# Weight conversion in pairs of slices, with the low parts formed by TensorE

## The chip, the cores and the metric

The kernel runs on one core of one Trainium2 chip. The metric is the device time of one execution in microseconds. The kernel before was timed in three runs: 685.75, 686.35 and 686.82 us, median 686.35. One execution was taken by the hardware profiler. Engines are named as in the profile: PE is TensorE's matmul (PEld its weight load), DVE is VectorE, ACT is ScalarE, POOL is GpSimd, SP is SyncE, which here issues nearly all transfers.

## The reference

The first stage is a linear attention with a complex decay, step by step over the sequence; the second is a feed-forward layer over its output.

```python
batch, n_heads, seq, head_dim = (4, 8, 768, 48)
n_tokens, d_model, d_ff = (3072, 384, 2048)

mag = np.sqrt(a_re * a_re + a_im * a_im)
scale = np.minimum(mag, 0.999) / (mag + 1e-06)
a_re_n, a_im_n = (a_re * scale, a_im * scale)
for t in range(S):
    ar, ai = (a_re_n[:, :, t, :, None], a_im_n[:, :, t, :, None])
    new_re = ar * S_re - ai * S_im
    new_im = ar * S_im + ai * S_re
    kv = np.einsum('bhd,bhe->bhde', k[:, :, t], v[:, :, t])
    S_re, S_im = (new_re + kv, new_im)
    y[:, :, t] = np.einsum('bhd,bhde->bhe', q[:, :, t], S_re)

h = x @ w_in          # x: y as (3072, 384)
g = np.maximum(0.01 * h, h)
out = g @ w_out
```

The two weight matrices come in as float64, 384 x 2048 and 2048 x 384.

## The kernel before

**Attention.** The sequence is cut into 6 chunks of 128 steps. A sub-step is one chunk of two of the four batches; there are 12, numbered n. For each, `prep(n)` normalises the decays and forms their running products, mostly on DVE with some steps on ACT (lines L422 to L540). It multiplies q and k by them into a tile `qkt` (L521, L533), which five transfers per real or imaginary part (L549, L553, L557) bring into the layout `t96` that PE needs. Then `attend(n, bi)` handles the two batches one by one: transposes (L588), scores (L601), the mask on DVE (L605), outputs and old state (L626), the new state (L639). The output is split into a high part `xh` (fp32r, ACT, L628) and a low part `xl` (DVE, L631).

**Feed-forward.** Two attended units, 256 tokens, make a group; there are 12 groups. `moe(g)` goes through the 2048 hidden columns two blocks of 128 at a time. `mm1` forms 18 matmuls into one of two PSUM buffers `ph` (L679 to L681: high by high, low by high, high by low part). ACT and DVE turn it into `gh` and `gl` (L685 to L688), and `mm2`, one step behind, adds 18 matmuls into three output buffers `po` (L696, L697, L702). At the end ACT copies them out (L715) and SP sends them (L716).

**Weights.** They arrive as 64-bit words, 32 slices of 128 x 384: 16 of `w_in`, 16 of `w_out`, in turn. `load_weights` makes an fp32 value of each slice: two bit operations on DVE (L378, L382), a conversion of the lower word on ACT (L385), an add on POOL (L386) into `wcv`. ACT rounds it to the high part (L387), and POOL subtracts that to get the low part (L388). Two `cvt` buffers hold slices under way. The raw words lie in buffers borrowed from other tiles (`a`, `kn`, `xh`, `xl`, and `stg`, which is also the output tile); from the tenth slice on, three of them rotate. Each slice is one transfer on SP (L323).

**What sets the order.** No order is written by hand. A scheduler gives each engine's instructions a fixed order by simulating the program: an instruction is placed when its inputs and buffers are ready there, and the ready one with the lowest number of priority comes first. The first loads have 0, attention 1,000,000, feed-forward 2,000,000, preparation n 3,000,000 + 10,000 n, weights 3,005,000, so all weights rank between the first and second preparation. Tiles of one tag share the tag's buffers; a new tile waits until the old one has been read for the last time. On the chip each engine and each queue then works through its list in order.

After the last attention `check_weights` and `flag` test the input ranges; a general version of the program stands behind a branch and does not run here.

## Time and profile before

| | |
|---|---|
| median of three runs | 686.35 us |
| profiled execution | 686.39 us |
| its span, first to last instruction | 684.3 us |
| granted TensorE clock, mean | 0.990 |
| busy: PE, DVE, ACT, POOL | 577.0, 550.2, 364.8, 78.0 us |
| POOL, subtracts L388 | 16 x 1.375 us and 16 x 1.223 us |
| second attention's preparation ends on DVE (L533) | 125.5 us |
| last high part of the weights (L387) ends | 150.8 us |
| first output copy of the first group (L715) | 170.6 us |

Rows of the profile name the line, the engine, the operation, the tile written and the tiles read, the shape, and the count. A row of the timeline starts with its start and its duration in us, and ends, in brackets, with the idle time of the engine before it and what ended that. A row of the groups gives busy time in all, the mean of one in ns, and the idle time before them.

### The profile page before, as it was taken

To read this page: it belongs to the slowest core of one execution; us is meant where nothing else is said; L and a number is where in the kernel's file an instruction comes from. 1 tells how busy PE (TensorE), PEld (TensorE's weight loads), DVE (VectorE), ACT (ScalarE), POOL (GpSimd) and SP (SyncE) were. 2 spreads that over 40 slices of the span, in tenths; PEclk is the share of its full clock that TensorE was granted. 3 is DMA by queue.
4 is the path that set the end of the run, shared out by engine and by line. 5 is a ranking of instruction groups with operands and counts; after the bars stand their busy time and mean duration, and the time that the engine had idled before them with its cause. 6 is when DMAs were issued, how large, how long until landed. Compare 5 with 4: busy or idle time off the path is not lost.

```text
span 684.3 us, 14080 instructions
## 1 busy us (share of the span) xinstructions
PE 577.0 (84%) x5732; PEld 555.4 (81%) x5732; DVE 550.2 (80%) x915; ACT 364.8 (53%) x815; POOL 78.0 (11%) x75
## 2 busy tenths in 40 slices
PE   0000475899999999999999999999999998999996
PEld 0000365798999899899999999989999997999996
DVE  5999899999989799898989989989889885233331
ACT  6245256457457275473755727538366277583321
POOL 5645255450000000000000000000000000000000
PEclk9999999999999999999999999999999999899998
DMA  8231733630421703408034070251701748750000
GB/s 329 78 103 69 217 107 119 151 129 29 110 100 52 186 15 88 136 29 209 8 86 145 28 187 25 69 146 51 184 4 51 210 166 194 269 196 13 24 1 29
DMA packets 26232, 74.27 MB, mean 109 GB/s; under 512 B 3376, under 2 KB 9520, under 8 KB 26160
## 3 DMA queue, kind: packets, MB, share of 16 engines
q1 hardware_dynamic: 25552, 71.71, 35.1%
q10 hardware_dynamic: 608, 1.59, 1.0%
q8 instruction: 47, 0.77, 0.5%
q14 instruction: 25, 0.20, 0.1%
HBM read 49.55 MB, written 4.72 MB: 79 GB/s over the span
## 4 chain that ended last, share of the span: by engine, by line
PE 45%; DVE 29%; DMA 12%; ACT 5%; issue 4%; SPq 2%; POOL 1%; ACTq 0%; DVEq 0%; POOLq 0%
DMA t<-qkt 6%; PE po L696 6%; PE po L697 6%; PE po L702 5%; DMA wck<-in_w_dram 5%; PE ph L679 5%; PE ph L680 5%; PE ph L681 5%; PE px L626 4%; PE ps L601 4%; PE pu L639 3%; DVE tg L686 2%; DVE tmp L443 2%; DVE wcv L378 2%; DVE gl L688 2%
## 5 line engine op out<-in xcount | busy, mean ns | idle before, releaser
L679 PE MATMUL ph<-xh,win_hi 128*128 128x256 f32 x576 | 165.2, 287 | 6.7 <-DVE tg L686 5.2
L680 PE MATMUL ph<-xl,win_hi 128*128 128x256 f32 x576 | 164.6, 286 | 2.7 <-DVE xl L631 2.7
L681 PE MATMUL ph<-xh,win_lo 128*128 128x256 f32 x576 | 164.0, 285 | 0.0
L696 PE MATMUL po<-gh,wout_hi 128*128 128x256 f32 x576 | 145.6, 287 | 0.5 <-ACT gh L687 0.5
L697 PE MATMUL po<-gh,wout_lo 128*128 128x256 f32 x576 | 144.8, 286 | 0.0
L679 PEld LDWEIGHTS ph<-xh,win_hi 128*128 128x128 f32 x576 | 110.0, 191 | 8.5 <-DVE tg L686 6.5
L680 PEld LDWEIGHTS ph<-xl,win_hi 128*128 128x128 f32 x576 | 110.1, 191 | 3.5 <-DVE xl L631 2.9
L696 PEld LDWEIGHTS po<-gh,wout_hi 128*128 128x128 f32 x576 | 110.3, 192 | 1.8 <-ACT gh L687 1.0
L697 PEld LDWEIGHTS po<-gh,wout_lo 128*128 128x128 f32 x576 | 110.5, 192 | 0.2 <-issue 0.2
L681 PEld LDWEIGHTS ph<-xh,win_lo 128*128 128x128 f32 x576 | 110.0, 191 | 0.0
L686 DVE TENSOR_TENSOR tg<-ph,tg 128x512 f32<-128x512 f32 x96 | 65.8, 688 | 53.4 <-ACT tg L685 51.0
L685 ACT ACTIVATE tg<-ph 128x512 f32<-128x512 f32 x96 | 57.2, 595 | 92.0 <-PE ph L681 80.0
L588 PE MATMUL ptk<-ident,t 96*128 96x96 f32 x160 | 24.9, 265 | 79.4 <-DMA t<-qkt 79.1
L702 PE MATMUL po<-gl,wout_hi 128*128 128x256 f32 x576 | 89.8, 287 | 0.1
L688 DVE TENSOR_TENSOR gl<-tg,gh 128x512 fp32r<-128x512 f32 x96 | 66.5, 697 | 28.7 <-ACT gh L687 20.2
L588 PEld LDWEIGHTS ptk<-ident,t 96*128 96x128 f32 x160 | 17.9, 150 | 83.6 <-DMA t<-qkt 78.4
L687 ACT CAST gh<-tg 128x512 fp32r<-128x512 f32 x96 | 59.2, 619 | 48.6 <-DVE tg L686 41.6
L702 PEld LDWEIGHTS po<-gl,wout_hi 128*128 128x128 f32 x576 | 77.5, 192 | 0.5 <-DVE gl L688 0.3
L601 PE MATMUL ps<-t 96*128 96x128 f32 x384 | 59.1, 298 | 6.9 <-DVE xl L631 4.2
L601 PEld LDWEIGHTS ps<-t 96*128 96x128 f32 x384 | 53.1, 210 | 8.1 <-DVE xl L631 4.4
L443 DVE TENSOR_TENSOR tmp<-a 128x384 f32<-128x384 f32 x84 | 51.5, 613 | 1.4
L626 PE MATMUL px<-asb,v 128*32 128x128 f32 x768 | 48.4, 288 | 0.8 <-DVE asb L605 0.8
(118 smaller groups left out, 953.1 us busy)
## 6 DMA issues: line engine op xcount, KB each, us to landing
t<-qkt SPq DMA_DIRECT2D x44, 290.2 KB, 5.4
wck<-in_w_dram SPq DMA_DIRECT2D x10, 1152.0 KB, 5.7
a<-in_a_dram SPq DMA_DIRECT2D x12, 768.0 KB, 6.1
qk<-in_qk_dram SPq DMA_DIRECT2D x12, 768.0 KB, 4.8
v<-in_v_dram SPq DMA_DIRECT2D x12, 448.0 KB, 3.3
out_dram<-ot SPq DMA_DIRECT2D x12, 384.0 KB, 2.6
stage_xh<-in_w_dram SPq DMA_DIRECT2D x10, 384.0 KB, 3.0
stage_xl<-in_w_dram SPq DMA_DIRECT2D x10, 384.0 KB, 3.2
```

The costliest lines, as they stand in the source:

```text
L443: nc.vector.tensor_tensor(out=pr, in0=src.unsqueeze(2).to_broadcast([P, 2, 2, M]), in1=swap(ar, r), op=ALU.mult)
L601: nc.tensor.matmul(ps[:, h4], lhsT=t96[:, slot_of(1, h), bi, 0:C], rhs=t96[:, slot_of(0, h), bi, 0:C], start=True, stop=True)
L626: nc.tensor.matmul(px[32 * q : 32 * q + 32, i], lhsT=lhsT, rhs=rhs, start=first, stop=last)
L679: nc.tensor.matmul(o, lhsT=win_hi[:, k, fs], rhs=xh[:, k, :nt], start=(k == 0), stop=False)
L680: nc.tensor.matmul(o, lhsT=win_hi[:, k, fs], rhs=xl[:, k, :nt], start=False, stop=False)
L681: nc.tensor.matmul(o, lhsT=win_lo[:, k, fs], rhs=xh[:, k, :nt], start=False, stop=(k == TI - 1))
L686: nc.vector.tensor_tensor(out=tg[:, :w], in0=ph[:, :w], in1=tg[:, :w], op=ALU.max)
L687: nc.scalar.copy(gh[:, :w], tg[:, :w])
L688: nc.vector.tensor_tensor(out=gl[:, :w], in0=tg[:, :w], in1=gh[:, :w].bitcast(F32), op=ALU.subtract)
L696: nc.tensor.matmul(po[o][:, :nt], lhsT=wout_hi[:, f, os], rhs=gh[:, ts], start=(f == 0), stop=False)
L697: nc.tensor.matmul(po[o][:, :nt], lhsT=wout_lo[:, f, os], rhs=gh[:, ts], start=False, stop=False)
L702: nc.tensor.matmul(po[o][:, :nt], lhsT=wout_hi[:, f, os], rhs=gl[:, ts], start=False, stop=(f == NFC - 1))
```

## The change

Two neighbouring slices of one matrix are converted together, so 16 transfers, 16 conversions of twice the width, and 16 high parts take the place of 32. POOL keeps the add. Its subtract goes. In its place PE forms, for each slice, identity times the fp32 value plus negated identity times the high part in a PSUM buffer of the tag `h`, the one that `ph` uses (two buffers), and ACT copies the result out as the low part. The negated identity `nid` is a new tile, made once by ACT.

The raw words now lie in one `a` buffer, the `qkt` buffer (two pairs) and two buffers `ws` of their own, which rotate from the sixth pair on. `xh`, `xl`, `kn` and `stg` no longer hold raw words. Space for this comes from a smaller scratch area of the program (`dynamic_dma_scratch_size`) and from merging two small tiles.

The first 8 pairs keep their priority behind the first preparation. The other 8 are called from `moe(0)`, two for each of its first four steps, and get 3,015,000: behind the second preparation.

```diff
-STAGES = [
-    ("a", 3 * TI * 2 * C, 2), ("kn", H * 2 * D, 1), ("xh", TI * GT, 2), ("xl", TI * GT, 2), ("xh", TI * GT, 2),
-    ("xl", TI * GT, 2), ("stg", 2 * DM, 1),
-]
-AHEAD = 4
-EARLY = 8
-def STAGE_OF(i):
-    return i if i < 9 else 6 + i % 3
+NWS = 2
+STAGES = [("a", 3 * TI * 2 * C, 2), ("qkt", 4 * TI * 2 * (C + 1), 1)] + [("ws", 4 * DM, NWS)] * NWS
+AHEAD = 2
+EARLY = 4
+FIRST = 8
+NROT = NWS
+def STAGE_OF(i, n):
+    return i if i < n else n - NROT + (i - n) % NROT
...
+    nid = cp.tile([P, P], F32R, tag="nid", name="nid")
...
+    nc.scalar.activation(nid, ident, AF.Copy, scale=-1.0)
...
-            loaded[i] = stage[STAGE_OF(i)]
-            nc.sync.dma_start(out=loaded[i].bitcast(I64), in_=w_in[i // 2 + NFC * (i % 2)])
+            loaded[i] = stage[STAGE_OF(i, len(stage))]
+            s0 = i // 2 * 2 + NFC * (i % 2)
+            nc.sync.dma_start(
+                out=loaded[i].rearrange("p (s x) -> p s x", s=2).bitcast(I64),
+                in_=w_in[s0 : s0 + 2].rearrange("s p x -> p s x"),
+            )
...
+        for i in range(lo, hi):
+            f = i // 2 * 2
+            st = weight_dma(i)
+            cv = pp.tile([P, 2 * DM], I32, tag="cvt", name=f"wcv_{i}", bufs=2)
...
             nc.scalar.activation(lo_w, uwords[:, :, 0], AF.Copy, scale=2.0**-29)
             nc.gpsimd.tensor_tensor(out=cv, in0=hi_w, in1=lo_w, op=ALU.add)
             nc.scalar.activation(dh, wf, AF.Copy)
-            nc.gpsimd.tensor_tensor(out=dl, in0=wf, in1=dh.bitcast(F32), op=ALU.subtract)
+            for x in range(2):
+                pd = psh.tile([P, 512], F32, tag="h", name=f"pd_{i}_{x}")[:, 0:DM].rearrange("p (k x) -> p k x", k=TI)
+                nc.tensor.matmul(pd, lhsT=ident, rhs=wf[:, x], start=True, stop=False)
+                nc.tensor.matmul(pd, lhsT=nid, rhs=dh[:, x], start=False, stop=True)
+                nc.scalar.copy(dl[:, x], pd)
...
         for f in range(0, NFC, nf):
+            if g == 0:
+                load_weights(min(FIRST + f, NFC), min(FIRST + f + 2, NFC), PRIO_PREP + 15_000)
+                prio(PRIO_MOE)
             cur = mm1(f)
...
     load(0)
-    load_weights(0, EARLY // 2, PRIO_PREP + 5_000)
+    load_weights(0, EARLY, PRIO_PREP + 5_000)
...
         if n == 0:
-            load_weights(EARLY // 2, NFC, PRIO_PREP + 5_000)
+            load_weights(EARLY, FIRST, PRIO_PREP + 5_000)
...
-    nc = bacc.Bacc("TRN2", target_bir_lowering=False, num_devices=1)
+    nc = bacc.Bacc("TRN2", target_bir_lowering=False, num_devices=1, dynamic_dma_scratch_size=1024)
```

More of the change, by code (lines that the diff above doesn't have):

```diff
@@ L275, in body @@
     xacc = keep.tile([P, NT // C], F32, tag="xacc", name="xacc")
-    low = keep.tile([P, 4], F32, tag="low", name="low")
+    low = keep.tile([P, 5], F32, tag="low", name="low")
+    low, lnc = low[:, 0:4], low[:, 4:5]
     zfl = keep.tile([P, nsub, 2 * TI], F32, tag="zfl", name="zfl")
-    lnc = cp.tile([P, 1], F32, tag="lnc", name="lnc")
     wacc = keep.tile([P, 2, WCP * -(-NWC // WCK)], F32, tag="wacc", name="wacc")
@@ L313, in body @@
         st = pp.tile([P, size], I32, tag=t, name=f"stage_{t}_{len(stage)}", bufs=nb)
-        stage += [st[:, i * 2 * DM : (i + 1) * 2 * DM] for i in range(size // (2 * DM))]
-    s_next = [0]
+        stage += [st[:, i * 4 * DM : (i + 1) * 4 * DM] for i in range(size // (4 * DM))]
     raw = {}
@@ new lines, in load_weights @@
+        for i in range(lo, hi):
+            f = i // 2 * 2
+            st = weight_dma(i)
+            cv = pp.tile([P, 2 * DM], I32, tag="cvt", name=f"wcv_{i}", bufs=2)
+            if i % 2 == 0:
+                dh, dl = (
+                    x[:, :, f * P : (f + 2) * P].rearrange("p k (s x) -> p s k x", s=2) for x in (win_hi, win_lo)
+                )
+            else:
+                dh, dl = (x[:, f : f + 2].rearrange("p s (k x) -> p s k x", k=TI) for x in (wout_hi, wout_lo))
+            words = st.rearrange("p (x two) -> p x two", two=2)
+            uwords = st.bitcast(U32).rearrange("p (x two) -> p x two", two=2)
+            hi_w, lo_w = words[:, :, 1], words[:, :, 0]
+            wf = cv.bitcast(F32).rearrange("p (s k x) -> p s k x", s=2, k=TI)
+            nc.vector.tensor_scalar(
+                out=cv.bitcast(U32), in0=uwords[:, :, 1], scalar1=5, scalar2=2,
+                op0=ALU.logical_shift_left, op1=ALU.logical_shift_right,
+            )
+            nc.vector.scalar_tensor_tensor(
+                out=hi_w, in0=hi_w, scalar=-(1 << 30), in1=cv, op0=ALU.bitwise_and, op1=ALU.bitwise_or
+            )
+            nc.scalar.activation(lo_w, uwords[:, :, 0], AF.Copy, scale=2.0**-29)
+            nc.gpsimd.tensor_tensor(out=cv, in0=hi_w, in1=lo_w, op=ALU.add)
+            nc.scalar.activation(dh, wf, AF.Copy)
+            for x in range(2):
[3 more added lines that the diff above has]
+                nc.scalar.copy(dl[:, x], pd)
```

25 lines of the change are left out of this document (removed).

## The prediction

> **What bounds the kernel now.** I read the busy shares over the span first, then the busy time by stages. The first view has one digit per 17.1 us, the share of the slice in tenths; the second gives start and end, length, and the busy time (and instruction count) of each engine.
>
> ```profile
> PE   0000475899999999999999999999999998999996
> DVE  5999899999989799898989989989889885233331
> POOL 5645255450000000000000000000000000000000
> ```
>
> ```profile
> core 0: us, PE busy (x) PEld busy (x) DVE busy (x) ACT busy (x) POOL busy (x), PEclk, DMA share, GB/s
> 0.00:77.70 77.70, 0.80 (x2) 0.50 (x2) 67.67 (x97) 33.15 (x63) 41.16 (x43) 1.00 0.42 145
> 77.70:109.50 31.80, 21.92 (x146) 18.48 (x146) 28.46 (x45) 18.91 (x49) 15.02 (x14) 1.00 0.48 162
> 109.50:171.00 61.50, 54.46 (x467) 52.11 (x468) 57.82 (x91) 35.41 (x83) 21.79 (x19) 0.97 0.35 103
> 171.00:684.30 513.30, 499.77 (x5118) 484.32 (x5117) 396.30 (x685) 277.30 (x621) 0.00 (x0) 0.99 0.35 100
> ```
>
> From 171 us to the end PE is busy 499.8 of 513.3 us, so the end stands about 513 us behind the end of the first feed-forward group. What the change can move lies before 171: there PE does almost nothing for 77.7 us, idles 9.9 us of the next 31.8 and 7.0 us of the 61.5 after that. Over the same 77.7 us DVE is busy 67.7, and GpSimd (POOL) works only in those early stages. The timeline shows who releases PE (in brackets the idle time before it and its releaser).
>
> ```profile
> 69.81 1.82 DVE L533 TENSOR_TENSOR qkt<-qk,a 128x768 f32<-128x768 f32 x2
> 77.71 0.58 PE L588 MATMUL ptk<-ident,t 96*128 96x96 f32 x2 [73.12 <-DMA t<-qkt]
> 94.75 3.78 PE L601 MATMUL ps<-t 96*128 96x128 f32 x16 [4.15 <-DVE xl L631]
> 109.52 0.58 PE L680 MATMUL ph<-xl,win_hi 128*128 128x256 f32 x1 [2.65 <-DVE xl L631]
> 170.62 0.63 ACT L715 COPY ot<-po 128x256 f32<-128x256 f32 x2
> ```
>
> The first preparation ends on DVE at 71.6, its relay through DMA releases PE at 77.7, and two later idle stretches (4.15 and 2.65 us) wait for DVE again. The ramp is bound by DVE; L715 at 170.6 is the end of group 0. DVE is not only full, it is stretched while POOL works. The groups of 0 to 72 us come first (busy, mean ns), then the same forms from 180 to 540 us, where POOL is silent.
>
> ```profile
> L443 DVE TENSOR_TENSOR tmp<-a 128x384 f32<-128x384 f32 x8 | 7.4, 930 | 0.1
> L437 DVE TENSOR_TENSOR a<-a,tmp 128x1536 f32<-128x1536 f32 x2 | 4.8, 2405 | 0.0
> L446 DVE TENSOR_TENSOR a<-tmp 128x192 f32<-128x192 f32 x7 | 3.8, 548 | 0.1
> L378 DVE TENSOR_SCALAR wcv<-stage_xl 128x384 uint32<-128x384 uint32 x5 | 3.2, 638 | 0.0
> L378 DVE TENSOR_SCALAR wcv<-stage_xh 128x384 uint32<-128x384 uint32 x5 | 3.2, 634 | 0.9 <-POOL win_lo L388 0.9
> L528 DVE TENSOR_TENSOR qk<-qk,a 128x768 f32<-128x768 f32 x1 | 1.8, 1750 | 0.0
> L378 DVE TENSOR_SCALAR wcv<-stage_stg 128x384 uint32<-128x384 uint32 x3 | 1.1, 353 | 0.0
> ```
>
> ```profile
> L443 DVE TENSOR_TENSOR tmp<-a 128x384 f32<-128x384 f32 x61 | 33.9, 556 | 1.0
> L446 DVE TENSOR_TENSOR a<-tmp 128x192 f32<-128x192 f32 x61 | 21.6, 354 | 0.9
> L437 DVE TENSOR_TENSOR a<-a,tmp 128x1536 f32<-128x1536 f32 x8 | 14.0, 1755 | 0.0
> L528 DVE TENSOR_TENSOR qk<-qk,a 128x768 f32<-128x768 f32 x8 | 7.6, 955 | 0.0
> L423 DVE SCALAR_TENSOR_TENSOR tmp<-tmp 128x768 f32<-128x768 f32 x8 | 7.6, 948 | 0.0
> ```
>
> Excess, count by difference of means: L443 8 x 0.37 = 3.0; L437 2 x 0.65 = 1.3; L446 7 x 0.19 = 1.4; L378 10 x 0.28 = 2.8 against its unstretched 0.353; L528 0.8. That is 9.3 us in 28 of the window's 87 DVE instructions. The rest hold single stretched ones like L528, so I take 16 us as an estimate for the whole stage: above 9.3, and well below the stage's POOL time of 41.2.
>
> Four more rows of the timeline date the steps that the parts below lean on.
>
> ```profile
> 24.07 0.82 POOL L386 TENSOR_TENSOR wcv<-stage_xl 128x384 int32<-128x384 int32 x1 [1.02 <-issue]
> 43.84 2.39 DVE L482 TENSOR_TENSOR qkt<-a 128x1536 f32<-128x1536 f32 x1
> 124.59 0.95 DVE L533 TENSOR_TENSOR qkt<-qk,a 128x768 f32<-128x768 f32 x1
> 150.30 0.53 ACT L387 ACTIVATE wout_hi<-wcv 128x384 fp32r<-128x384 f32 x1
> ```
>
> **The change, part by part.** POOL, from the groups by line (min/median/max ns of one):
>
> ```profile
> L386 POOL TENSOR_TENSOR wcv<-stage_xh x10: 823/849/1470, 22.2 to 146.1; 128x384 int32<-128x384 int32 x10
> L388 POOL TENSOR_TENSOR win_lo<-wcv,win_hi x16: 990/1034/2535, 10.4 to 150.2; 128x384 fp32r<-128x384 f32 x16
> ```
>
> Per slice POOL holds 0.82 (add) + 0.99 (subtract) = 1.81 us undisturbed. All 32 subtracts go. The add on twice the width isn't in the trace; its cost lies between one add of today (0.82, if width were free) and two (1.65). I take 1.55, near two, since L388's and L386's times are all of one width and show no large fixed part. Per slice that is 0.78: 57% of POOL's net time goes, and I let the stretch go with it: 16 x 0.57 = 9 us before PE's start (bounds 5, from the 9.3 shown alone, and 13, if short stretches vanish).
>
> A rule of the Trainium skill speaks to this. "SBUF — State Buffer", section "SBUF: two separate sides", has VectorE and GpSimd share one port pair as an exclusive lock that is held for a whole instruction, against VectorE instructions with two SBUF inputs or in a two-port mode. The stretched L443, L437 and L528, whose two inputs both lie in SBUF, agree. By the rule alone a wider add blocks for twice as long at a time, and the case where nearly all of it lands on DVE is the third rival below.
>
> DVE's own weight work: 16 slices before PE starts cost 16 x (0.35 + 0.55) = 14.4 us now. Afterwards 8 x (L378 wide + L382 wide). L382 wide is a two-input instruction of 768 columns like L423: 0.95. L378 wide lies between 0.35 and 0.70; I take 0.55. Together 12.0, so 2.4 less, of which I give 0.4 back because a filler of 0.95 us delays a ready preparation step longer than one of 0.55. Sum before PE's start: -11 us.
>
> In 77.7 to 109.5, POOL is busy 15.0 us, 36% of the 41.2 of the first stage; the same ratio gives a stretch of 5.8 and a saving of 3.3. Part of the second-half conversions fall here too and must pass DVE, which is below the attention in priority but not always behind it: I take -3 (bounds 0 and -6). From 109.5 to 171, POOL's 21.8 us give a saving of 4.8 on DVE, but PE idles only 7.0 there and is otherwise full: -2 (bounds 0 and -5).
>
> What is added on PE, with the rows that price it: the critical chain (start, us) for a warm fp32 matmul, recorded as two passes of 128 columns each, and for the fp32r one of 256 columns; ACT groups behind them, and last a row of PE's waits (us, times, longest).
>
> ```profile
> 290.04 0.89 PE ps L601 x8
> ```
>
> ```profile
> 611.97 0.72 PE po L702 x6
> ```
>
> ```profile
> L593 ACT COPY kn<-ptk 128x384 f32<-128x384 f32 x40 | 19.0, 474 | 47.6 <-PE ptk L588 47.6
> L424 ACT ACTIVATE tmp<-tmp 128x768 f32<-128x768 f32 x12 | 10.1, 846 | 4.6 <-DVE tmp L423 4.6
> L387 ACT ACTIVATE win_hi<-wcv 128x384 fp32r<-128x384 f32 x16 | 8.4, 522 | 13.3 <-POOL wcv L386 13.3
> L385 ACT ACTIVATE stage_xl<-stage_xl 128x384 int32<-128x384 uint32 x10 | 5.6, 558 | 1.6 <-DMA stage_xl<-in_w_dram 1.6
> ```
>
> ```profile
> PE ph L679 <- DVE tg L686: 5.2, 5, 2.9
> ```
>
> An fp32 pass takes 0.89 / 8 = 0.111 per 128 columns, so the identity product on 384 columns takes 2 x 3 x 0.111 = 0.67. The fp32r product takes 0.72 / 6 = 0.12 per 256, so 0.18 for 384. One low part: 0.85 us of PE, 27 us for all 32. The first 16 run while PE waits (idle 73.12 above): free, even at the slow pace of L601 at 94.75 (3.78 / 16 = 0.236 a pass, twice 0.111). If that cover were gone they would cost 13.6. The other 16, 13.6 us, run between PE's start and the end of group 0. There PE idles 9.9 + 7.0 = 16.9 us today, so they cost between 0 and 13.6; I take half, 6.8, because the placing puts them where DVE also has room.
>
> ACT per two slices: now 2 x (0.56 + 0.52) = 2.16; after, two at 0.85 (L424's form) and two PSUM copies of 0.47 (L593's), 2.64. Eight us more over the whole conversion on an engine busy 33 of 77.7: nothing, with that idle time as cover. If it had none, 16 x 0.48 = 7.7 us.
>
> New waits: the low parts take turns with ph in two PSUM buffers. Behind a low part's matmul, PE's queue holds the group's own matmuls and the next attention, and its buffer comes back only after ACT's copy. Today ph already waits 5.2 us for L686 in all. The added wait lies between 0 and 16 x 0.47 = 7.6 (each copy uncovered); I take 2.5.
>
> DMA: 16 issues of twice the size for 32, the same bytes, all on SP. The rotation now uses stages of its own, so xh, xl, kn and ot no longer wait for weights; qkt does, for the second and third pair, on which the first preparation's L482 at 43.8 depends. Today the sixth slice is through its add by 24.9, so 19 us cover it: nothing. The second activation loads (a) wait for one pair, not three slices: nothing. One negated identity on ACT at the start: nothing, ACT waits for its first input.
>
> Sum: -11 - 3 - 2 + 6.8 + 2.5 = **-6.7 us**. The profiled execution took 686.39 (span 684.3 and 2.1 around it), 0.04 from the median 686.35: 679.7.
>
> **The rivals.** (1) *Nothing added is felt*: DVE has so much room that the second half is converted before group 0 needs it, in PE's idle time, and does not run inside the group at all. Then 6.8 and 2.5 fall away and the early preparation gains some 2 more: 668. For it: 16.9 us of idle PE. Against: the second half stands behind the second preparation in priority.
>
> (2) *Two PSUM buffers for two users* (slower). Place: group 0. If each of the 16 low parts makes PE stand for its copy and half an ACT instruction ahead of it (0.47 + 0.4) as well as its 0.85, that is 16 x 1.72 = 27.5 against the 16 gained: 698. It decides from 16 - 13.6 = 2.4 us of waiting, 0.15 us a low part, if no low part is hidden, and from 0.57 us a part where half are. For: PE is in order, ACT too. Against: mm2's 18 matmuls (18 x 0.12 = 2.2 us) stand between two ph and need no such buffer.
>
> (3) *The wide add blocks DVE for its whole length*: 8 x 1.55 = 12.4 of stretch before PE's start instead of 7: the gain falls from 16 to about 9, and 9.3 us are added: 686.7, no change. This is the lock of the Trainium skill's "SBUF — State Buffer" taken strictly. Against: today 15 slices' POOL time by 72 us, 27 us undisturbed, stretches DVE by about 16, not 27.
>
> (4) *Late weights*. The second half stands behind the second preparation, and today that ends on DVE near 125. If its eight steps run at 6 us each from 115, weights arrive at 163 instead of about 150, and group 0 ends near 175 instead of 170.6: 691. For: conversion, matmul and copy are now seven steps on four engines. Against: each step needs only 1.5 us of DVE, and two buffers overlap.
>
> **How the numbers follow.** Forecast 0.46 (679.7, own range 673 to 685); rival 1, 0.14 (668); rival 2, 0.17 (698); rival 3, 0.13 (686.7); rival 4, 0.10 (691). The range is 667 to 695: it takes in rivals 1, 3 and 4, the bounds of the stretch, and the nearer part of rival 2; about 0.15 is left out, most of it above. About 0.2% (1.4 us) is what a measurement of this kernel can tell from no change. Faster: 0.45 of the forecast, rival 1, and 0.02 of rival 3, 0.61. Slower: rivals 2 and 4 and 0.03 of rival 3, 0.30. Same: 0.09.
>
> **What would show it.** First PE work after the mask near 66 to 68 instead of 77.7, and L443 near 0.75 us there instead of 0.93. POOL busy about 30 us in all, not 78. The first ph near 95; L715 of group 0 near 164. Low-part matmuls of the first half with PE idle around them; those of the second with PE gaps ahead of them rather than behind. After group 0 the same 513 us as now. Wrong if PE starts at 75 or later (the stretch is not POOL's subtracts), if PE's idle time before the end of group 0 grows over 17 us with ACT's low copy as releaser (rival 2), if L387 still releases ph late (rival 4), or if the stage after group 0 changes its length by more than 4 us.

## The result, and the profile after

The changed kernel takes 708.4 us (median of four runs, 707.1 to 710.4); the kernel before, run beside it, takes 686.6. The ratio is 1.032, with a 95% interval from 1.029 to 1.035. The forecast was 679.7 with a range from 667 to 695. The profiled execution took 707.08 us, its span is 705.4, 21.1 us longer than before. Medians and ratios leave out executions that the chip ran in a slower state, four of e17_early_own's twelve (up to 769.9 us) and one of e16_early_relay_own's ten.

First the busy shares of the changed kernel, 17.6 us to a digit.

```profile
PE   2753297968999999999989999899999989999996
DVE  5999596898797987978979899798998733333331
POOL 3323100100000000000000000000000000000000
```

PE now works from the start (the low parts), DVE has holes from the fifth slice on, and POOL is nearly silent: 31.5 us in all, 78.0 before. So the load did leave POOL and DVE, and yet the kernel is slower. The stretches say where. Columns as in the prediction: start and end, length, busy time (count) of PE, PEld, DVE, ACT and POOL. The cuts are PE's first attention work and the end of group 0's output copies. First the kernel before:

```profile
77.70:171.60 93.90, 76.99 (x618) 71.18 (x619) 86.88 (x136) 54.92 (x135) 36.82 (x32) 0.98 0.39 123
171.60:684.30 512.70, 499.17 (x5114) 483.72 (x5112) 395.70 (x684) 276.70 (x619) 0.00 (x0) 0.99 0.35 100
...
77.70:684.30 606.60, 576.16 (x5730) 554.90 (x5730) 482.58 (x819) 331.62 (x752) 36.82 (x32) 0.99 0.36 104
```

Then the changed kernel; the last row counts the low parts' instructions alone, so its columns are PE, PEld and ACT:

```profile
0.00:82.25 82.25, 33.43 (x62) 17.00 (x62) 69.09 (x93) 47.02 (x77) 25.60 (x23) 0.72 0.55 183
82.25:191.60 109.35, 94.56 (x740) 83.46 (x741) 88.94 (x148) 57.68 (x143) 5.87 (x4) 0.79 0.33 99
191.60:705.40 513.80, 491.89 (x5029) 476.46 (x5027) 374.00 (x643) 270.42 (x598) 0.00 (x0) 0.99 0.33 94
...
82.25:705.40 623.15, 586.46 (x5766) 559.93 (x5766) 462.94 (x790) 328.10 (x739) 5.87 (x4) 0.96 0.33 95
...
82.25:705.40 623.15, 14.93 (x36) 7.61 (x36) 5.89 (x12) 0.96 0.33 95
```

The rest after group 0 is 513.8 against 512.7 us, so the end of group 0 comes 20.0 of the 21.1 us later. PE's start comes 4.55 us later (82.25 against 77.70), where 11 us earlier was forecast. After its start PE is busy 10.3 us longer (586.46 against 576.16: 14.93 more for low parts, 4.6 less for all else), and idle 6.3 us longer (623.15 - 586.46 = 36.7 against 30.4). The sum is 21.1.

The idle time does not grow inside group 0: there it is 14.8 us (109.35 - 94.56) against 16.9 (93.90 - 76.99), and after it 21.9 (513.80 - 491.89) against 13.5 (512.70 - 499.17). Nor does the cut at the group's end part equal work: by then the changed kernel has 86 passes of the attention's score products in that stretch (L608), the kernel before 64 (L601). So the rest of the changed kernel has 7.3 us less PE work and 8.4 us more idle time, and its like length is no sign that nothing changed there.

Two stretches of the changed kernel's timeline carry the rest of this text. The first is the end of the first preparation and its relay (start, duration, engine, line; in brackets the idle time before and its end):

```profile
63.34 9.87 SPq L325 DMA_DIRECT2D stage_ws<-in_w_dram  x2
68.40 4.41 POOL L389 TENSOR_TENSOR wcv<-stage_ws 128x768 int32<-128x768 int32 x1 [5.09 <-DVE stage_ws L385]
69.41 1.81 DVE L540 TENSOR_TENSOR qkt<-qk,a 128x768 f32<-128x768 f32 x2
72.85 0.84 ACT L390 ACTIVATE wout_hi<-wcv 128x768 fp32r<-128x768 f32 x1 [4.39 <-POOL wcv L389]
72.91 1.26 ACTq L556 DMA_DIRECT2D t<-qkt  x2
73.30 2.32 SPq L556 DMA_DIRECT2D t<-qkt  x2
82.26 0.58 PE L595 MATMUL ptk<-ident,t 96*128 96x96 f32 x2 [20.66 <-DMA t<-qkt]
```

The preparation (L540, L533 before) ends on DVE at 71.2 us, only 0.4 earlier than before. Its transfers on ACT's queue stand behind L390, which waits 4.39 us for a wide add on POOL; those on SP's queue stand behind two weight transfers whose issue ends at 73.2. From DVE's end to PE's start it takes 11.0 us, 6.1 before.

The second is the conversion of the weights itself:

```profile
62.43 0.46 ACT L395 CAST wout_lo<-pd 128x384 fp32r<-128x384 f32 x1
63.34 0.84 ACT L390 ACTIVATE win_hi<-wcv 128x768 fp32r<-128x768 f32 x1 [0.45 <-POOL wcv L389]
106.66 0.58 PE L686 MATMUL ph<-xh,win_hi 128*128 128x256 f32 x1 [1.58 <-ACT xh L635]
107.04 1.48 PE L393 MATMUL pd<-wcv,ident 128*128 128x384 f32 x2
108.88 0.48 ACT L395 CAST win_lo<-pd 128x384 fp32r<-128x384 f32 x1 [2.13 <-PE pd L394]
114.66 1.47 POOL L389 TENSOR_TENSOR wcv<-stage_ws 128x768 int32<-128x768 int32 x1 [41.85 <-DMA t<-qkt]
148.38 1.62 PE L393 MATMUL pd<-wcv,ident 128*128 128x384 f32 x2 [4.95 <-ACT wout_lo L395]
191.00 0.62 ACT L725 COPY ot<-po 128x256 f32<-128x256 f32 x2
```

Twelve pairs pass DVE by 71.2 us; ten pairs' low parts are copied by 62.9. Then no low part comes for 46 us, and POOL adds nothing for 41.85. The eleventh pair has its high part at 64.2 (L390), and the product for its low part runs at 107.04, right behind the first product of group 0 at 106.66. PE idles from 61.6 to 82.3 in between, so neither the input nor a busy PE holds that product back.

### The profile page after: what moved, and what is told of

The parts are those of the page before. It is cut to its first block, busy times and chain, and to the rows that moved or that the text cites. A ratio compares the mean times of both kernels' runs of the same rounds, so it can differ in the third digit from the quotient of the medians.

```text
span 705.4 us, 14138 instructions
## 1 busy us (share of the span) xinstructions
PE 619.9 (88%) x5828; PEld 576.9 (82%) x5828; DVE 532.0 (75%) x883; ACT 375.1 (53%) x816; POOL 31.5 (4%) x27
## 3 DMA queue, kind: packets, MB, share of 16 engines
q1 hardware_dynamic: 25296, 71.71, 33.9%
## 4 chain that ended last, share of the span: by engine, by line
PE 38%; DVE 34%; DMA 13%; ACT 6%; issue 5%; SPq 3%; POOL 0%; ACTq 0%; DVEq 0%; POOLq 0%
DMA wck<-in_w_dram 6%; DMA t<-qkt 5%; PE po L703 5%; PE po L704 5%; PE po L709 4%; PE ph L686 4%; PE ph L688 4%; PE ph L687 4%; PE px L633 3%; PE ps L608 3%; DVE tg L693 3%; DVE gl L695 3%; DVE tmp L450 3%; PE pu L646 2%; DVE a L494 2%
## 5 line engine op out<-in xcount | busy, mean ns | idle before, releaser
L703 PE MATMUL po<-gh,wout_hi 128*128 128x256 f32 x576 | 142.7, 284 | 1.4 <-ACT gh L694 0.7
L704 PE MATMUL po<-gh,wout_lo 128*128 128x256 f32 x576 | 141.9, 283 | 0.0
L703 PEld LDWEIGHTS po<-gh,wout_hi 128*128 128x128 f32 x576 | 108.5, 189 | 3.0 <-ACT gh L694 0.9
L704 PEld LDWEIGHTS po<-gh,wout_lo 128*128 128x128 f32 x576 | 108.6, 189 | 0.2 <-issue 0.2
L709 PE MATMUL po<-gl,wout_hi 128*128 128x256 f32 x576 | 87.7, 284 | 0.2 <-DVE gl L695 0.2
L709 PEld LDWEIGHTS po<-gl,wout_hi 128*128 128x128 f32 x576 | 75.9, 188 | 1.1 <-DVE gl L695 0.4
L393 PE MATMUL pd<-wcv,ident 128*128 128x384 f32 x64 | 39.4, 735 | 28.1 <-POOL wcv L389 17.9
L608 PE MATMUL ps<-t 96*128 96x128 f32 x384 | 60.3, 301 | 3.9 <-DMA t<-qkt 2.9
L608 PEld LDWEIGHTS ps<-t 96*128 96x128 f32 x384 | 54.1, 212 | 5.0 <-DMA t<-qkt 3.3
L595 PE MATMUL ptk<-ident,t 96*128 96x96 f32 x160 | 26.4, 278 | 34.0 <-DMA t<-qkt 33.8
L612 DVE TENSOR_TENSOR asb<-ps,mask 128x512 f32<-128x512 f32 x48 | 32.7, 685 | 27.4 <-PE ps L608 27.2
```

Source lines behind the costliest of these rows:

```text
L595: nc.tensor.transpose(out=pt[:, h4, 0:96], in_=t96[:, slot_of(1, hh * 4 + h4), bi, 0:C], identity=ident[0:96, 0:96],)
L608: nc.tensor.matmul(ps[:, h4], lhsT=t96[:, slot_of(1, h), bi, 0:C], rhs=t96[:, slot_of(0, h), bi, 0:C], start=True, stop=True)
L703: nc.tensor.matmul(po[o][:, :nt], lhsT=wout_hi[:, f, os], rhs=gh[:, ts], start=(f == 0), stop=False)
L704: nc.tensor.matmul(po[o][:, :nt], lhsT=wout_lo[:, f, os], rhs=gh[:, ts], start=False, stop=False)
L709: nc.tensor.matmul(po[o][:, :nt], lhsT=wout_hi[:, f, os], rhs=gl[:, ts], start=False, stop=(f == NFC - 1))
```

## The experiments

One table first. Each row's time is the median of its runs, the ratio is to the kernel before on the same chip. The other columns come from the profiled execution, from the windows cut at PE's first attention work: that start, PE's time in low parts after it, PE's time in all else, PE's idle time after it. The four add up to the span.

| kernel | us | ratio (95%) | start | low parts | other | idle |
|---|---|---|---|---|---|---|
| before | 686.6 | 1 | 77.7 | 0 | 576.2 | 30.4 |
| changed | 708.4 | 1.032 (1.029 to 1.035) | 82.3 | 14.9 | 571.5 | 36.7 |
| e1_pool_sub | 696.2 | 1.012 (1.008 to 1.017) | 90.7 | 0 | 572.6 | 32.0 |
| e2_pe_only | 697.2 | 1.016 (1.012 to 1.020) | 74.7 | 22.4 | 565.0 | 33.5 |
| e3_no_pe | 672.2 | 0.980 (0.975 to 0.986) | 78.0 | 0 | 568.2 | 24.8 |
| e4_all_early | 681.5 | 0.991 (0.988 to 0.995) | 83.4 | 10.1 | 562.0 | 25.6 |
| e9_rank_only | 701.2 | 1.019 (1.012 to 1.025) | 81.5 | 15.7 | 568.8 | 33.9 |
| e10_place_only | 684.5 | 0.996 (0.993 to 0.999) | 83.3 | 9.9 | 563.1 | 25.2 |
| e5_after_relay | 691.1 | 1.006 (1.004 to 1.009) | 68.3 | 19.9 | 568.5 | 32.3 |
| e8_early_relay | 699.3 | 1.016 (1.010 to 1.023) | 68.4 | 21.4 | 565.8 | 42.0 |
| e7_att_buf | 711.3 | 1.036 (1.033 to 1.040) | 73.8 | 19.0 | 574.8 | 41.3 |
| e13_own_buf | 682.1 | 0.991 (0.987 to 0.994) | 72.6 | 16.1 | 560.9 | 31.0 |
| e14_att_two | 705.8 | 1.027 (1.023 to 1.031) | 81.5 | 14.3 | 569.9 | 38.0 |
| e6_half | 688.1 | 1.003 (1.000 to 1.005) | 88.2 | 0 | 565.6 | 32.3 |
| e11_relay_half | 682.1 | 0.993 (0.990 to 0.996) | 68.4 | 0 | 575.0 | 37.1 |
| e12_early_relay_half | 681.4 | 0.991 (0.987 to 0.995) | 68.5 | 0 | 576.2 | 37.2 |
| e15_relay_own | 687.4 | 1.000 (0.998 to 1.003) | 68.1 | 19.5 | 564.3 | 31.5 |
| e16_early_relay_own | 689.1 | 1.003 (1.000 to 1.005) | 68.3 | 18.8 | 564.3 | 35.7 |
| e17_early_own | 680.9 | 0.990 (0.987 to 0.994) | 72.7 | 16.1 | 558.5 | 27.0 |
| e18_before_warm | 686.5 | 0.999 (0.996 to 1.001) | 79.4 | 0 | 570.7 | 33.2 |

### Which part of the change costs: e1, e2, e3

e1_pool_sub, in the changed kernel:

```diff
...
-                nc.tensor.matmul(pd, lhsT=ident, rhs=wf[:, x], start=True, stop=False)
-                nc.tensor.matmul(pd, lhsT=nid, rhs=dh[:, x], start=False, stop=True)
-                nc.scalar.copy(dl[:, x], pd)
+                nc.gpsimd.tensor_tensor(out=dl[:, x], in0=wf[:, x], in1=dh[:, x].bitcast(F32), op=ALU.subtract)
```

> The changed kernel with one part undone: the low part is a GpSimd subtract on two 384-column halves again, the rest (pairs, own stages, second half ranked inside group 0) stays. Theory B (the 21.1 us of span are mostly the products on PE and the waits for their two PSUM buffers): PE's busy time after its start falls from 586.5 to about 576, the 5 us gap behind the low copy at 143 goes, and the time is near 692 even though GpSimd stretches DVE more. Theory A (the late first attention is what costs, from weight pairs that run ahead and from queues held by the wide add): PE starts at 84 or later, since GpSimd now holds DVE and the queues longer, and the time stays at 704 or above.

Each theory got one half. PE starts at 90.7, as A has it: the first preparation's last multiplies (L537 in this kernel) end on DVE at 84.5, two of them 3.08 us long from 81.39. What follows the start is 604.6 us, 2.0 less than before, as B has it. So pairs with their place in the order cost 13 us of start even with the subtracts on GpSimd; and since this kernel starts 8.5 us later than the changed one and is still 12 us faster, the products on PE are a second loss.

e2_pe_only, in the kernel before, with the tile `nid` and the smaller scratch area of the change:

```diff
...
-                nc.gpsimd.tensor_tensor(out=dl, in0=wf, in1=dh.bitcast(F32), op=ALU.subtract)
+                pd = psh.tile([P, 512], F32, tag="h", name=f"pd_{s}")[:, 0:DM].rearrange("p (k x) -> p k x", k=TI)
+                nc.tensor.matmul(pd, lhsT=ident, rhs=wf, start=True, stop=False)
+                nc.tensor.matmul(pd, lhsT=nid, rhs=dh, start=False, stop=True)
+                nc.scalar.copy(dl, pd)
```

> The kernel before with one part done alone: one slice at a time, the old stages and order, but the low parts are two PE products into the feed-forward's PSUM buffers and an ACT copy. Theory A (pairs and their place in the queues make PE start late): here no wide add stands on GpSimd, so PE starts before 77.7, at about 73, and the kernel pays only for the low parts that run after it (at most 16 of 32, 0.8 us each, near 10): about 690. Theory B/C (the products and their buffers make the whole loss): 698 to 705, with PE starting near 77 all the same. If the relief of DVE was never real, PE's start stays at 77 to 78.

The start is 74.7, near A's 73, so relieving POOL does bring PE forward. The time, 697.2, is just under B's 698. PE's first feed-forward product comes at 133.96 us; before it came at 106.07. Every low part stands ahead of it.

e3_no_pe, in the changed kernel; the low parts of the weights are left out, ACT writes zeros:

```diff
...
-                nc.tensor.matmul(pd, lhsT=ident, rhs=wf[:, x], start=True, stop=False)
-                nc.tensor.matmul(pd, lhsT=nid, rhs=dh[:, x], start=False, stop=True)
-                nc.scalar.copy(dl[:, x], pd)
+            nc.scalar.activation(dl[:, x], wf[:, x], AF.Copy, scale=0.0)
```

> The changed kernel with the low parts of the weights left out of the computation: ACT writes zeros of the same size in place of the copies from PSUM, and neither the products on PE nor their PSUM buffers exist; the feed-forward's own products keep their number. What PE and PSUM cost is the difference to the changed kernel. Theory B/C: 10.3 us of PE work and at least the 5 us gap go, so 690 to 694. Theory A: PE still starts at 81 to 83, 4.5 us later than before, so it stays above 690 by no more than that. If the products cost nothing (they lie in idle time), it stays at 706 to 709.

708.4 - 672.2 = 36 us go, about twice what B and C priced. The profiled executions differ by 34.4: by the table 14.9 are the products themselves, 11.9 PE's idle time, 4.3 the start and 3.3 PE's other work. The start, 78.0, is earlier than A's 81 to 83, so the products cost something ahead of it too.

### Rank or place: e4, e9, e10

e4_all_early: all sixteen pairs in front of the second preparation, none in group 0.

```diff
-FIRST = 8
+FIRST = 16
```

> The changed kernel with all sixteen pairs ranked in front of the second preparation, none inside group 0, so only the place in the order changes. Theory A (pairs that run ahead of the first attention delay it): four more pairs may run ahead, PE starts at 83 to 86, but fewer low parts fall into PE's full stretch; 702 to 710, no clear change. Rival (the place inside group 0 is what costs, through weights that come late): the 5 us gap at 143 goes and group 0 ends at 180 or earlier, for 695 to 700.

A foresaw no gain, and the other theory less of one. With the late start unchanged (83.4) the kernel is 27 us faster than the changed one and beats the kernel before. The two things that FIRST changes were then taken apart. e9_rank_only:

```diff
-                load_weights(min(FIRST + f, NFC), min(FIRST + f + 2, NFC), PRIO_PREP + 15_000)
+                load_weights(min(FIRST + f, NFC), min(FIRST + f + 2, NFC), PRIO_PREP + 5_000)
```

> The changed kernel with one number changed: the second half of the weights stays inside group 0 in the code, but gets the rank of the first half (in front of the second preparation) in place of the rank behind it. Theory R (the rank is what costs: the second half converts behind the second preparation, PE waits and turns cold, and its low parts land in PE's full stretch): the last low part comes near 110 to 115 as with all pairs early (110), and the time is 679 to 686. Theory S (the place in the code costs, as transfers and copies are issued inside the group): 700 or more, little changed.

e10_place_only:

```diff
             load_weights(EARLY, FIRST, PRIO_PREP + 5_000)
+            load_weights(FIRST, NFC, PRIO_PREP + 15_000)
...
-            if g == 0:
-                load_weights(min(FIRST + f, NFC), min(FIRST + f + 2, NFC), PRIO_PREP + 15_000)
-                prio(PRIO_MOE)
```

> The changed kernel with the second half called right behind the first half in the code, but with the rank that it has inside group 0 (behind the second preparation). Theory R (the rank costs): no gain, the last low part stays near 155 and the time at 702 to 712. Theory S (the place in the code costs): 679 to 690.

It is the place in the code, in the main. Rank alone gives 7 of the 27 us, place alone 24. ACT's rows of e9_rank_only show the same hole as the changed kernel's, of e10_place_only the last low parts before 112 and group 0's end near 169:

```profile
61.99 0.46 ACT L395 CAST wout_lo<-pd 128x384 fp32r<-128x384 f32 x1
106.72 0.48 ACT L395 CAST win_lo<-pd 128x384 fp32r<-128x384 f32 x1 [1.16 <-PE pd L394]
```

```profile
110.87 0.90 ACT L395 CAST wout_lo<-pd 128x384 fp32r<-128x384 f32 x2
168.13 0.92 ACT L722 COPY ot<-po 128x256 f32<-128x256 f32 x3
```

### The late start: e5, e8

e5_after_relay: in SP's queue the second half's transfers stand behind the first relay's last transfer of its first plane (the first of the real and the imaginary part).

```diff
-            nc.sync.dma_start(
+            with tc.issue_after(first_relay[0]) if i >= FIRST else ExitStack():
+                nc.sync.dma_start(
...
+            if n == 0 and l == 0:
+                first_relay.append(getattr(last, "ins", last))
```

> The changed kernel with one order added: the transfers of the second half's pairs stand behind the first relay's last transfer of its first plane in SP's queue. So none of these pairs can run ahead of the first attention. Theory A (the run-ahead pairs and the queues that they hold ate the relief of DVE): PE's first attention work falls from 82.3 to 74 to 77, at most what DVE's 5 us of weight work and the 5 us longer relay give. Rival (DVE's own work ahead of the first attention sets it): it stays at 80 or later. The time itself need not gain, since the second half only comes later: 698 to 712.

```profile
60.34 1.83 DVE L542 TENSOR_TENSOR qkt<-qk,a 128x768 f32<-128x768 f32 x2
61.36 1.24 SPq L558 DMA_DIRECT2D t<-qkt  x2
68.35 0.55 PE L599 MATMUL ptk<-ident,t 96*128 96x96 f32 x2 [20.43 <-DMA t<-qkt]
```

The start comes at 68.35, earlier than A asked for. The first preparation ends at 62.2 on DVE, 9.0 us before the changed kernel's 71.2, and the relay takes 6.2, 4.9 less. Eight pairs pass DVE by then, twelve in the changed kernel. So the relief of DVE was there, and the pairs that ran ahead ate nearly all of it: rank decides only among what is ready, and a pair whose data have come fills every moment in which the preparation waits. Which of ACT's and SP's queue held the relay was not tried by itself. After the start little changed: 620.7 us in place of 623.15, so the gain, 17.3 us in all, is mostly the start's 13.9; 691.1 is below the 698 to 712 that I expected.

e8_early_relay is the same on top of e4_all_early:

```diff
-FIRST = 8
+FIRST = 16
...
+            with tc.issue_after(first_relay[0]) if i >= 8 else ExitStack():
```

> All pairs ranked in front of the second preparation (the run that took 681.5, PE's start 83.4), with the transfers of pairs 8 to 15 behind the first relay's last transfer of its first plane in SP's queue. Theory A: PE starts at 74 to 77, and if the later pairs still end before 120, the time is 673 to 678. Rival (the pairs that run ahead are needed early): PE starts earlier, but then idles for the late pairs, 681 to 690.

The start holds, the time is worse than both expectations. ACT's last low copy and PE's first feed-forward product of this kernel:

```profile
131.00 0.48 ACT L397 CAST wout_lo<-pd 128x384 fp32r<-128x384 f32 x1 [0.35 <-PE pd L396]
```

The first feed-forward product follows at 132.46; in e2_pe_only, too, it came only behind the last low part, and in the changed kernel the eleventh pair's low part came only behind the first feed-forward product. All three follow the order in the code, whatever was ready. That gave a new theory: a tag's PSUM buffers are handed out in the order of the code, so in two shared buffers low parts and feed-forward products take turns, and who is late holds up the other.

### Turns in the shared buffers: e7, e13, e14

e7_att_buf, in the changed kernel:

```diff
-                pd = psh.tile([P, 512], F32, tag="h", name=f"pd_{i}_{x}")[:, 0:DM].rearrange("p (k x) -> p k x", k=TI)
+                pd = psa.tile([P, 512], F32, tag="att", name=f"pd_{i}_{x}")[:, 0:DM].rearrange("p (k x) -> p k x", k=TI)
```

> The changed kernel with the low parts' products in the attention's three PSUM buffers in place of the feed-forward's two. Theory C (two buffers for two users, the second rival of the prediction): the gap of 4.95 us behind the low copy and the two short ones of 0.7 go, for 700 to 703. Theory D (the copies are late because ACT's queue is held by what stands ahead of them, so any buffer waits): a gap of like size stays behind the copy or moves to the attention's own products, and the time stays within 3 us of 708.

No gain, as D says, but not for D's reason alone. Group 0 ends at 162.5, 29 us earlier than in the changed kernel, and then the rest takes longer:

```profile
73.80:162.50 88.70, 78.18 (x519) 66.76 (x520) 78.56 (x121) 50.73 (x109) 12.75 (x6) 0.81 0.35 108
162.50:708.90 546.40, 515.60 (x5261) 497.06 (x5260) 391.93 (x676) 283.25 (x638) 0.00 (x0) 0.98 0.34 93
```

546.4 us in place of 513, with PE waiting 10.8 us for two relays between 200 and 300. Theory C's 700 to 703 did not come. It does not answer the question, since the low parts only take turns with the attention now. The start is 73.8, though, with nothing done to the transfers. So a buffer of their own, e13_own_buf; it is taken from the attention, which keeps two of three:

```diff
-    psa = ctx.enter_context(tc.tile_pool(name="psa", bufs=3, space=bass.MemoryType.PSUM))
+    psa = ctx.enter_context(tc.tile_pool(name="psa", bufs=2, space=bass.MemoryType.PSUM))
+    psd = ctx.enter_context(tc.tile_pool(name="psd", bufs=1, space=bass.MemoryType.PSUM))
...
-                pd = psh.tile([P, 512], F32, tag="h", name=f"pd_{i}_{x}")[:, 0:DM].rearrange("p (k x) -> p k x", k=TI)
+                pd = psd.tile([P, 512], F32, tag="pd", name=f"pd_{i}_{x}")[:, 0:DM].rearrange("p (k x) -> p k x", k=TI)
```

> The changed kernel with one PSUM buffer of their own for the low parts' products, taken from the attention (two in place of three). Theory T (turns): in the shared buffers the low parts of pair 10 and later stand in turn behind the first feed-forward product, as they do in the code; in the changed kernel no low part came between 63 and 108.9 us for that reason. Then here low parts come in that stretch too, the last near 115 to 130 in place of 157.5, and the time is 685 to 697 (more if two attention buffers cost, which the next run shows alone). Rival (rank and readiness make them late, not turns): the gap from 63 to about 105 and the last low part near 155 stay, and the time stays at 705 or above.

e14_att_two has only the first line of that diff:

> Control for the run before: the changed kernel with two attention buffers in place of three and nothing else. PE's attention alternates products and copies, so two buffers may cost some PE idle time in each attention: 708 to 716, with the last low part near 155 as in the changed kernel. Less than 708 would mean that the run before cannot be read as the effect of the own buffer alone.

The control is 705.8, the own buffer 682.1: 23.7 us by the buffer alone. The control missed its 708 from below, so two attention buffers in place of three cost no time, and by its own words e13 can't be read against the changed kernel: the control is what it is compared with here. The own buffer's time is also under the 685 that Theory T had for its best. The hole is gone (ACT's and POOL's rows of e13_own_buf, then group 0's end; the control below):

```profile
64.77 0.48 ACT L396 CAST win_lo<-pd 128x384 fp32r<-128x384 f32 x1 [1.38 <-PE pd L395]
75.94 0.48 ACT L396 CAST win_lo<-pd 128x384 fp32r<-128x384 f32 x1
84.73 1.47 POOL L390 TENSOR_TENSOR wcv<-stage_ws 128x768 int32<-128x768 int32 x1 [12.61 <-DVE xs L474]
163.72 0.92 ACT L726 COPY ot<-po 128x256 f32<-128x256 f32 x3
```

```profile
61.91 0.47 ACT L395 CAST wout_lo<-pd 128x384 fp32r<-128x384 f32 x1
110.04 0.50 ACT L395 CAST win_lo<-pd 128x384 fp32r<-128x384 f32 x1
182.50 0.42 ACT L725 COPY ot<-po 128x256 f32<-128x256 f32 x1
```

One part of the expectation was wrong: the last low part still ends at 158, not at 115 to 130. So its lateness is not what made the changed kernel slow. That the turns cost through what they hold up (`wcv` buffers, POOL, PE's queue) fits the rows, but was not tried one by one. The start moves too, to 72.6, with nothing done to the transfers' order: ten pairs pass DVE by the end of the first preparation (66.7 us), twelve by its end in the control (70.7), and the relay takes 5.9 us in place of 10.8. In e7_att_buf, too, it is ten pairs and an early start (73.8). So in both runs PE's start comes forward when the low parts leave the feed-forward's buffers; why fewer pairs run ahead then stays open.

### Both at once, and what is left: e6, e11, e12, e15 to e18

e6_half puts the second half's low parts on POOL; e11_relay_half adds e5's order, e12_early_relay_half that of e8:

```diff
+            if i < FIRST:
...
+            else:
+                for x in range(2):
+                    nc.gpsimd.tensor_tensor(out=dl[:, x], in0=wf[:, x], in1=dh[:, x].bitcast(F32), op=ALU.subtract)
```

> The changed kernel with the second half's low parts as GpSimd subtracts (two of 384 columns a pair), the first half's still on PE. The second half's 4 pairs that run ahead then hold GpSimd before PE's first attention, the others stretch DVE inside group 0. Theory B (the second half's products in PE's queue are the larger loss): 14.9 us of PE work after the start and the gap of 4.95 go, PE's start stays near 82 to 85, for 685 to 692. If the loss is only the late start: 700 or more.

> Both causes taken away at once: the second half's transfers stand behind the first relay (PE's start 68.35 in that run), and its low parts are GpSimd subtracts, the first half's on PE. If the two causes are separate and make up the loss: start near 68, none of the 19.9 us of products after it, GpSimd's stretch on DVE as in the kernel before (about 5 us) in place of them: 670 to 680, faster than both kernels. If PE after its start only waits for late weights in another way: 685 or more.

> As the run before it, but with the second half ranked and called in front of the second preparation, as in the kernel before. Weights come earlier and the second preparation later. Start near 68; 668 to 678 if GpSimd's stretch of DVE is what it was, 680 to 690 if PE waits at group 0 for the second half (that run with products on PE waited 13.3 us for the wide add).

e6 came as B has it, 20 us under the changed kernel although it starts at 88.2, later than the 82 to 85 expected: no product on PE stands in group 0 any more. e11 and e12 are faster than the kernel before, but at 682 and 681 they miss their 670 to 680 and 668 to 678 (e12 falls into its other range, 680 to 690), and gain less than the start at 68.4 promised (it alone is 9.3 us): PE idles 37 us after it, 7 more than before, in group 0 mostly for DVE (in e11 6.8 us at once for `tg`, a tile that DVE makes of `ph`), which now is what follows too slowly.

e15_relay_own and e16_early_relay_own join the own buffer with the order of e5 and of e8 (the diffs are those above):

> Both causes with the products kept on PE: the second half's transfers behind the first relay (PE's start 68.35, 691.1 us with shared buffers) and the low parts in a PSUM buffer of their own. Theory T: the last low part comes before 130 (145.5 with shared buffers), the waits of 9.8 us for the low copies go, 678 to 686. Rival: 689 or more, since the low parts still are 20 us of PE work after the start.

> All pairs called and ranked in front of the second preparation, the second half's transfers behind the first relay, and the own PSUM buffer. With shared buffers this took 699.3 us, and the first feed-forward product came at 132.5, behind the last low part at 131.0, as the turns have it. Theory T: the first feed-forward product comes at 96 to 110 now, ahead of the last low parts, and the time falls to 676 to 688. Rival (PE's own order and the wide adds hold it): the first feed-forward product stays behind 125 and the time above 693.

Both cures do not add: 687.4 and 689.1, slower than the own buffer alone and outside Theory T's 678 to 686 and 676 to 688. e16 confirms the turns in one point: its first feed-forward product comes at 98.8 in place of 132.5, and it is ten us faster than with shared buffers. Holding back the transfers makes the second half later, and 16 low parts (19 us of PE) fall behind the start in place of 14; the last of them ends at 184 in e15, where Theory T had it before 130.

e17_early_own is the own buffer with FIRST = 16:

> All pairs called and ranked in front of the second preparation (681.5 us with shared buffers, PE's start 83.4) and the low parts in a PSUM buffer of their own (682.1 with the second half inside group 0, start 72.6), no order added for the transfers. If turns are the one cause of the loss: 678 to 686, since with all pairs early they already stood ahead of the first feed-forward product. If the own buffer also brings PE's start forward by itself (81.5 to 72.6 in its run against the control): start near 73 and 670 to 676.

0.990 with an interval from 0.987 to 0.994, as good as e4 and e13 and not to be told from them. The start is 72.7 as in e13 (83.4 with shared buffers), as the second theory has it, but the time is that of the first: 680.9, not 670 to 676. Its row of the table is from an execution of 676.0 us, one of its fastest.

e18_before_warm, in the kernel before, adds products whose result is unused:

```diff
+        if n == 0:
+            warm = psa.tile([P, 4, P], F32, tag="att", name="warm")
+            for _ in range(11):
+                nc.tensor.matmul(warm[:, 0:3], lhsT=ident, rhs=qk[:, 1, 0:384], start=True, stop=True)
```

> The kernel before with one thing added: eleven identity products of 384 columns on PE, their result unused, that can start when the first preparation's last multiply but one is done (69.4 us) and fill the wait until 77.7. PE's own work after its start is 576.2 us there and 561 to 563 in the runs where its products reach 0.12 us a pass early. Theory P (the slow pace ends once PE has been busy for some 10 to 20 us): score products at 0.12 to 0.14 us a pass by 90 in place of 0.24 at 94.75, work after the start down to 565 to 572, 677 to 684. Rival (the pace there is granted by time or by something else): 0.24 at 94 still, and 686 to 688.

```profile
69.49 10.06 PE L532 MATMUL warm<-qk,ident 128*128 128x384 f32 x22 [64.88 <-DVE qk L528]
81.76 1.98 PE L605 MATMUL ps<-t 96*128 96x128 f32 x16
91.69 3.49 PE L605 MATMUL ps<-t 96*128 96x128 f32 x16 [2.02 <-DVE xl L635]
```

The first attention runs at 0.124 us a pass (1.98 / 16), the second at 0.218 (3.49 / 16); before, the second took 0.236 (3.78 / 16 at 94.75). The time is that of the kernel before. PE's work falls by 5.5 us, its idle time grows by 2.8 and its start comes 1.7 later. Theory P's 677 to 684 did not come: the faster first attention only waited for what followed, as its rows wait for DVE (L635). The fast pace did not last, either: from 92 to 108 us the granted clock is 0.50 in this run, and the second attention is slow again. So a smaller "other" in the table need not shorten the time, and what a fast pace throughout would be worth was not tried.

## Why the prediction was wrong, point by point

**Prices.** Those on DVE and POOL held; a low part's on PE did not (below). These are rows of the changed kernel, min/median/max in ns:

```profile
L381 DVE TENSOR_SCALAR wcv<-stage_ws x13: 544/551/1636, 20.2 to 140.2; 128x768 uint32<-128x768 uint32 x13
L385 DVE SCALAR_TENSOR_TENSOR stage_ws<-stage_ws,wcv x13: 943/950/961, 21.8 to 141.0; 128x768 int32<-128x768 int32 x13
L389 POOL TENSOR_TENSOR wcv<-stage_ws x13: 1465/1467/4413, 23.1 to 142.2; 128x768 int32<-128x768 int32 x13
```

0.55 and 0.95 were forecast, and 1.55 for the add. The stretch on DVE fell as forecast as well: L450 (L443 before) has a mean of 0.713 us up to 71 us, where 0.75 was forecast and 0.930 stood before. The groups of the changed kernel's DVE up to 71.2 us:

```profile
L381 DVE TENSOR_SCALAR wcv<-stage_ws 128x768 uint32<-128x768 uint32 x9 | 6.0, 670 | 0.5 <-PE pd L393 0.5
L450 DVE TENSOR_TENSOR tmp<-a 128x384 f32<-128x384 f32 x8 | 5.7, 713 | 0.1
...
L381 DVE TENSOR_SCALAR wcv<-stage_qkt 128x768 uint32<-128x768 uint32 x2 | 1.1, 552 | 0.0
...
L381 DVE TENSOR_SCALAR wcv<-stage_a 128x768 uint32<-128x768 uint32 x1 | 0.6, 552 | 0.0
```

**"Sum before PE's start: -11 us"** failed first, by 15.6 us (+4.55 came). The step that failed is "Afterwards 8 x (L378 wide + L382 wide)": twelve pairs passed DVE before the first preparation ended (x9, x2 and x1 of L381 above), not eight, because the second half's rank behind the second preparation does not keep a ready pair from filling a gap in the first. With eight, in e5, the start is 68.35, against 66.7 by the sum. The second part of it is a wait for which the sum has no term: the relay took 4.9 us longer, behind L390 and two weight transfers.

**"I take half, 6.8"** and **"I take 2.5"** failed by 12.2 us together with the gains of 3 and 2 after the start: that stretch was to grow by 4.3 and grew by 16.5 (606.6 to 623.15). Twelve low parts took 14.93 us, 1.24 each where 0.85 was taken, and PE's idle time grew by 6.3 where it was to shrink (inside group 0 it did, by 2.1; it grew behind it). The step that failed is the cost of sharing two buffers, taken as waits for copies of at most 7.6 us. Against its control e13 gains 23.7 us by a buffer of their own, though the low parts still cost 16.1 us of PE after the start: by the table the start is 8.9 us earlier, the idle time 7.0 less, PE's other work 9.0 less. These three were not varied apart. 15.6 and 12.2 are the 27.8 us by which the span, 705.4, is over the forecast's (679.7 less the 2.1 around it).

**The rivals.** Rival 2 named the place, two PSUM buffers for two users, and a slower kernel, but its price was PE standing for a copy and half an ACT instruction at each low part, 698. What decides is the order in which the buffers are handed out: the eleventh pair waits 43 us (64.2 to 107.04) for group 0's first product, not half a microsecond for a copy. "mm2's 18 matmuls stand between two ph", the argument against it, is true and beside the point. Rival 4 said late weights; the last low part is as late in e13, which is faster than the kernel before. Rival 3 did not come: L450 fell. The rule of the Trainium skill ("SBUF — State Buffer", section "SBUF: two separate sides") that it rested on is borne out by single rows only: L389 takes 1.467 us in the median and 4.41 at 68.40, where DVE runs L540 beside it. No run varied the width of the add alone.

**Held:** POOL's 31.5 us (30 forecast) and one sign that would make the forecast wrong: PE started later than 75. The 513.8 us after group 0 (513 forecast) held by luck, with 7.3 us less PE work and 8.4 more idle time in them. The sign for rival 2 did not come: PE idles 14.8 us before the end of group 0, not over 17, of which 4.95 at 148.38 wait for the low copy.

## What to carry to other kernels

A new user of a rotating buffer takes its turn in the order of the code, and its rank hardly helps it (7 of 27 us here); put its call where its turn should come, or give it a buffer of its own (here one number, FIRST = 16, turns 1.032 into 0.991). Work moved behind something by rank alone still runs ahead of it as soon as it is ready, and then holds the engine and the queues that the urgent work needs: count what can run early, not what should. A relief is worth what the next engine can use of it: two cures of 17 and 24 us did not add.

## What the runs showed of the hardware

PE's pace after its start was not foreseen. The changed kernel's scores and state products, from PE's timeline:

```profile
96.15 3.78 PE L608 MATMUL ps<-t 96*128 96x128 f32 x16 [0.66 <-ACT kn L600]
103.58 1.50 PE L633 MATMUL px<-asb,v 128*32 128x128 f32 x20
```

and of e13_own_buf:

```profile
79.72 1.97 PE L609 MATMUL ps<-t 96*128 96x128 f32 x8
82.78 1.08 PE L634 MATMUL px<-asb,v 128*32 128x128 f32 x32
```

The changed kernel still runs at 0.236 us a pass 14 us after its start, with no gap over 1.05 us since, and at 0.075 for a product of L633 at 103.58; e13 reaches 0.034 for it ten us after its start, where low parts of 128 x 128 x 384 stand between the attention's smaller products. What ended the slow pace elsewhere was a run of feed-forward products: they start 0.21 us apart at first and 0.12 apart from 111.6 on in the changed kernel (first of them at 106.66), from 113.7 in the kernel before (109.52) and from 109.0 in e18 (104.18), after 4 to 5 us each. The Trainium skill ("TensorE: Matmul & The Clock Gate", section "What's actually happening") gives some 3.4 us of activity for the change to the fast pace; the feed-forward products come near it, the attention's products in the changed kernel do not agree. That dense products are what counts would fit all four kernels, but no run varied that alone.

The granted clock has to be read with care. These are its rows on the two kernels' profile pages, one digit per slice as for the busy shares, the changed kernel first:

```profile
PEclk9965556989999999999999999999999999999999
PEclk9999999999999999999999999999999999899998
```

In the changed kernel the clock follows the pace from 82 us on: windows of 2 us read 0.50 from 82 to 110 and 1.00 from 112 to 114. In the kernel before it reads 1.00 in all windows from 60 to 134, though the products are as slow up to 113.5: L608 and L601 take the same 3.78 us for 16 passes. So 1.00 at the beginning of a profile does not show a fast PE, and the mean clocks of the two kernels, 0.93 and 0.99, do not compare their pace.
